# Which softmax heads VectorE computes: a fixed list per head group, or two heads of a key tile ahead when counted time allows

## The chip, the cores and the metric

The kernel runs on one core of one Trainium2 chip. The metric is device time in microseconds (us), from one execution's start to its end on the device; lower is better. "The time" is the median of several executions; a profile shows one execution.

## The reference

Four layers in a row on x of shape (1, 2048, 640) in bf16: attention, token mixer, attention, token mixer, each with a layer norm in front and a residual sum behind. Both attention layers use the same weights, both mixers too.

```python
def _A_ref(x, wqkv, wo):                     # attention, H = 32 heads, Dh = 20
    qkv = (x @ wqkv).reshape(B, S, 3, H, Dh) # then transposed to q, k, v of (B, H, S, Dh)
    scores = einsum("bhqd,bhkd->bhqk", q, k) * (Dh ** -0.5)
    o = einsum("bhqk,bhkd->bhqd", softmax(scores), v)
    return o.transpose(...).reshape(B, S, D) @ wo

def _B_ref(x, w1, b1, w2, b2):               # mixes along the 2048 tokens, F = 1536
    u = gelu(einsum("bsd,sf->bdf", layernorm(x), w1) + b1)
    return (einsum("bdf,fs->bds", u, w2) + b2).transpose(0, 2, 1)

x = x + A(layernorm(x)); x = x + B(layernorm(x)); x = x + A(layernorm(x)); x = x + B(layernorm(x))
```

With 32 heads and 2048 x 2048 scores a head, each attention layer has 134 million exponentials.

## The kernel before

**Tiling.** The 32 heads lie in 8 groups `g` of 4 heads `j`, each padded from 20 to 32 columns, so that a group fills 128 partitions. The queries are cut into 4 blocks `qb` of 512, the keys into 16 tiles `kt` of 128. A *unit* is one (qb, g, kt): 4 heads, each a 128 x 512 block of scores (keys on the partitions, queries along the row). A layer has 512 units and 2048 such heads; they are worked through in the order qb, g, kt. A unit's four score matmuls (line 468) use 32 rows of TensorE each; the four matmuls of exp(scores) with V (line 704, with a column of ones for the softmax's denominator) use 32 columns each and add up in one PSUM accumulator `acc` over the group's 16 key tiles.

**Tiles for ScalarE.** Heads for ScalarE are packed into tiles of three and two heads in turn, each width with one PSUM buffer (`sps`). One activation (line 499) computes the exponentials of a tile and writes `P` to SBUF.

**Heads for VectorE.** Some heads go to VectorE instead. Their scores land in a PSUM buffer of their own (`Dt`, one buffer). VectorE computes the exponential for two heads at a time: one read of each head from PSUM (line 346, `ew`), and then a chain of four instructions on both (lines 387 `ey`, 393 `et`, 400 and 405 `Pd`): the fraction's polynomial, and the exponent added as bits. Which heads these are is fixed: `on_ve(n, j)` names all four heads of the group's last key tile, and heads 2 and 3 of the last but one in the first query block and in 11 of the 24 other groups. That is 166 heads a layer.

**The order of the work.** The program is written tile by tile in one Python loop, and all matmuls are chained in that order on TensorE. For each tile `t` the loop emits the scores of tile t+1 (`emit_S`, with `ve_admit` at its end, which may add one VectorE head), the activation of tile t, up to two units' P x V (`pv_next`, `emit_PV`), then "fills": matmuls of other work from `fill_queue`, such as the projections of K and Q, the output projection and the first half of the mixer for finished query blocks. Where too little is left for TensorE, zero matmuls are added (`keep_busy`, line 489). At the end of a step `ve_step` moves a *counted clock* on by the tile's counted length (1.344 or 0.92 us) and emits the VectorE chain's next instructions as far as that clock lets them start. Every VectorE instruction adds its counted duration through `dve_cost`. Nothing of this is measured while the kernel runs: it only fixes the order of the instructions.

- `ve_admit(t)` takes the next head of the fixed list at the earliest every second tile (`VE_SPACING`). In the first query block a group's heads are taken only once the group has started, later from 24 ScalarE heads ahead (`VE_LEAD`). A backlog of over 3.6 us (`VE_BACKLOG`), or a `Dt` that is not yet read by the counted clock, holds it back, unless the heads are `urgent`, near the group's end.
- `pv_next` takes plain units first and the mixed ones (those with VectorE heads) at the group's end.
- `ve_flush` emits what is left of a unit's chain when its P x V is emitted.
- After a group's last P x V, `normalize` reads the accumulator (line 507, a 32 x 32 block transpose), takes the reciprocals (510), multiplies (512) all 32 columns of each head's block by them into `T2`, and transposes back into `attnT` (514). The next group's P x V starts two tiles later (`ACC_REST`); it needs the same accumulator buffer.
- A fill's result is copied out of PSUM by VectorE (663 for K and Q, 578 for the mixer, 610 to 648 for the output projection). The mixer's results go from `ustg` (two buffers) to memory by DMAs from the GpSimd queue (581, and 583 with accumulation).

The two mixer stages lie between and behind the attention layers and are not touched.

## Time and profile before

| what | value |
|---|---|
| three runs | 2001.93, 2007.28, 2008.22 us; median 2007.28 |
| the profiled execution | 2002.34 us, of which its span 2000.5 |
| busy, share of the span | TensorE 91%, ScalarE 90%, VectorE 70%, GpSimd 8% |
| first attention stage, 49 to 918 us | 869 us; ScalarE 854.48, VectorE 629.59 busy |
| between: mixer and projections, 918 to 1047 us | 129 us |
| second attention stage, 1047 to 1917 us | 870 us; ScalarE 851.20, VectorE 623.10 busy |
| exponentials on ScalarE (499) | 1506 instructions, 1718.6 us busy, 33.1 us idle before them |
| exponentials on VectorE (346, 387, 393, 400, 405) | 332 heads, 947.4 us busy |
| granted TensorE clock | 0.992 |

The span runs from the first to the last instruction of the profiled execution. Busy time is the union of an engine's instructions. A busy TensorE is partly the zero matmuls, and matmuls of different rows or columns of the array overlap. Idle time "before" a group is what the engine stood idle just ahead of these instructions, with the work that ended the longest part of it.

### The profile page before, as it was taken

What the parts mean: (1) busy time and instruction counts of PE and PEld (TensorE: products, weight loads), DVE (VectorE), ACT (ScalarE), POOL (GpSimd) and SP (SyncE); (2) the same over time, 40 slices, a digit from 0 to 9 for tenths busy, and PEclk for the clock granted to TensorE, in tenths of its full rate; (3) what the DMA queues carried; (4) which work ended last, traced back from release to release, by engine and by line L of the source; (5) the groups of instructions that cost most, each with busy time, mean ns of one, the idle gap of its engine ahead of it and who ended that gap; (6) DMA issues with size and microseconds to landing.
All of it is one profiled execution on the core that took longest, in us unless ns stands there. A gap on an engine that the chain in (4) does not pass through costs nothing.

```text
span 2000.5 us, 41377 instructions
## 1 busy us (share of the span) xinstructions
PE 1819.5 (91%) x17472; PEld 619.9 (31%) x17472; DVE 1399.3 (70%) x2091; ACT 1810.2 (90%) x1644; POOL 155.1 (8%) x220
## 2 busy tenths in 40 slices
PE   7999999999999999897999989999999998998979
PEld 4222222322222222223542222323222222322235
DVE  6777787766776577773667787877657765767742
ACT  5999999999999999996349999999999999999952
POOL 2000000100021001100000000001000310111000
PEclk9999999999999999999999999999999999999989
DMA  6000001200143012314620000112001520222055
GB/s 136 2 1 1 1 21 35 81 26 9 33 84 53 1 46 46 45 15 141 205 85 1 1 1 1 47 39 77 13 21 56 77 38 2 71 52 39 7 154 183
DMA packets 90777, 97.47 MB, mean 49 GB/s; under 512 B 9696, under 2 KB 68192, under 8 KB 90592
## 3 DMA queue, kind: packets, MB, share of 16 engines
q1 hardware_dynamic: 70464, 71.22, 11.5%
q0 software_dynamic: 20128, 23.62, 7.6%
q8 instruction: 136, 2.23, 0.5%
q14 instruction: 49, 0.40, 0.1%
HBM read 55.48 MB, written 39.32 MB: 47 GB/s over the span
## 4 chain that ended last, share of the span: by engine, by line
ACT 29%; issue 25%; DVE 21%; PE 20%; POOL 3%; DMA 2%; SPq 0%; POOLq 0%; ACTq 0%; DVEq 0%
ACT P L499 29%; PE y L943 5%; PE S L468 4%; DVE et L393 3%; DVE ew L346 3%; DVE Pd L400 3%; DVE Pd L405 2%; PE acc L704 2%; POOL uacc L583 2%; PE misc L245 2%; PE acc L489 2%; DVE ey L387 2%; PE pp L236 1%; DVE T L507 1%; DVE KT L663 1%
## 5 line engine op out<-in xcount | busy, mean ns | idle before, releaser
L499 ACT ACTIVATE P<-S 128x1536 bf16<-128x1536 f32 (+1 forms) x1506 | 1718.6, 1311 | 33.1 <-PE S L468 27.2
L468 PE MATMUL S<-QTq,KT 32*128 32x512 bf16 x3764 | 593.3, 383 | 85.5 <-ACT P L499 75.0
L489 PE MATMUL acc<-zr,zw 128*32 128x512 bf16 x6112 | 484.2, 384 | 0.0
L346 DVE TENSOR_SCALAR ew<-Dt 128x512 int32<-128x512 f32 x332 | 226.3, 682 | 286.9 <-PE Dt L468 279.0
L704 PE MATMUL acc<-P,Vaug 128*32 128x512 bf16 x3764 | 383.4, 390 | 22.1 <-DVE T L507 21.5
L468 PEld LDWEIGHTS <-KT 32*128 32x128 bf16 x4096 | 192.5, 91 | 652.4 <-issue 631.6
L393 DVE SCALAR_TENSOR_TENSOR et<-ey 128x1024 f32<-128x1024 f32 x166 | 202.5, 1220 | 4.1
L400 DVE SCALAR_TENSOR_TENSOR Pd<-et,ey 128x1024 bf16<-128x1024 f32 x166 | 202.0, 1217 | 2.7
L405 DVE SCALAR_TENSOR_TENSOR Pd<-ew,Pd 128x1024 int16<-128x1024 int16 x166 | 201.9, 1216 | 2.6
L704 PEld LDWEIGHTS <-Vaug 128*32 128x32 bf16 x4096 | 108.6, 93 | 268.9 <-issue 264.6
L489 PEld LDWEIGHTS <-zw 128*32 128x32 bf16 x6112 | 140.7, 96 | 124.2 <-issue 75.3
L187 POOL TENSOR_TENSOR rstd<-veps,mhalf 128x1 f32<-128x1 f32 x64 | 38.9, 608 | 1248.3 <-DVE veps L182 1127.2
L468 PE MATMUL Dt<-QTq,KT 32*128 32x512 bf16 x332 | 126.7, 382 | 6.4 <-DVE ew L346 5.7
L572 PE MATMUL misc<-h2st,w1st 128*128 128x512 bf16 (+1 forms) x576 | 115.3, 302 | 10.1 <-DVE ustg L578 9.4
L578 DVE COPY ustg<-misc 128x512 f32<-128x512 f32 (+1 forms) x144 | 69.4, 482 | 76.9 <-PE misc L572 39.2
L387 DVE TENSOR_SCALAR ey<-ew 128x1024 f32<-128x1024 uint16 x166 | 114.7, 691 | 3.4
L583 POOL DMA_DIRECT2D uacc<-ustg x96 | 86.2, 908 | 346.7 <-DVE ustg L578 318.7
L943 PE MATMUL y<-uT,w2s 128*128 128x512 bf16 (+1 forms) x768 | 107.9, 299 | 2.6 <-ACT uT L886 2.6
L245 PE MATMUL misc<-hh,wq_pad 128*128 128x512 bf16 x310 | 94.2, 384 | 8.6 <-DVE KT L663 6.1
L245 PE MATMUL misc<-hh,wk_pad 128*128 128x512 bf16 x280 | 83.8, 383 | 7.5 <-DVE KT L663 7.4
L507 DVE STREAM_TRANSPOSE T<-acc 128x512 f32<-128x512 f32 x64 | 45.4, 710 | 57.3 <-PE acc L704 57.0
L600 PE MATMUL misc<-wo_pad,attnT 128*128 128x512 bf16 (+1 forms) x384 | 76.1, 303 | 0.5 <-DVE xin L610 0.2
(89 smaller groups left out, 959.2 us busy)
## 6 DMA issues: line engine op xcount, KB each, us to landing
uacc<-ustg POOLq DMA_DIRECT2D x72, 256.0 KB, 4.1
w2s<-in_B_w_dram SPq DMA_DIRECT2D x16, 768.0 KB
w1st<-in_B_w_dram SPq DMA_DIRECT2D x36, 256.0 KB
x1in<-xd SPq DMA_DIRECT2D x24, 320.0 KB
ua<-uacc SPq DMA_DIRECT2D x24, 320.0 KB
xd<-x2s SPq DMA_DIRECT2D x16, 320.0 KB
xin<-xd SPq DMA_DIRECT2D x16, 320.0 KB
uacc<-ustg POOLq DMA_DIRECT2D x72, 64.0 KB, 3.1
```

The source lines that it names most:

```text
L245: pe(nc.tensor.matmul(t[:, :], lhsT=wpad[:, dt_, g, :], rhs=st.hT[:, dt_, tb * 512:(tb + 1) * 512], start=(dt_ == 0), stop=(dt_ == NDT - 1)))
L346: nc.vector.tensor_scalar(out=ve_w[p][:, slot, :], in0=Dt[:, :], scalar1=ve_scale * 65536.0, scalar2=-127.0 * 65536.0, op0=ALU.mult, op1=A ...
L387: nc.vector.tensor_scalar(out=y[:, 0:512 * k], in0=frac, scalar1=EXP_K / 65536.0, scalar2=EXP_K * (1.0 - EXP_ROOT), op0=ALU.mult, op1=ALU.add)
L393: nc.vector.scalar_tensor_tensor(out=box["t"][:, 0:512 * k], in0=y, scalar=EXP_P, in1=y, op0=ALU.add, op1=ALU.mult)
L400: nc.vector.scalar_tensor_tensor(out=box["P"], in0=box["t"][:, 0:512 * k], scalar=EXP_Q, in1=box["y"][:, 0:512 * k], op0=ALU.add, op1=ALU. ...
L405: nc.vector.scalar_tensor_tensor(out=bits, in0=whole, scalar=128.0, in1=bits, op0=ALU.mult, op1=ALU.add)
L468: pe(nc.tensor.matmul(out_ap, lhsT=KT[32 * j:32 * j + 32, g, kt * 128:(kt + 1) * 128], rhs=get_QT(st, qb)[32 * j:32 * j + 32, g, :], start ...
L489: pe(nc.tensor.matmul(acc[32 * j:32 * j + 32, :], lhsT=zw[:], rhs=zr[:].to_broadcast([128, 4, 128]), start=False, stop=False, skip_group_c ...
L499: nc.scalar.activation(out=P[:, 0:ncs, :].rearrange("p a b -> p (a b)"), in_=St[:, 0:ncs, :].rearrange("p a b -> p (a b)"), func=ACT.Exp, ...
L583: nc.gpsimd.dma_start(out=dst, in_=stg[:, 0:w], accum_op=ALU.add)
L704: pe(nc.tensor.matmul(acc[32 * j:32 * j + 32, :], lhsT=Vaug[:, (kt * H + hh) * VW:(kt * H + hh) * VW + 32], rhs=P[:, slot, :], start=(done ...
L943: pe(nc.tensor.matmul(y[:, 0:w], lhsT=w2s[:, ft, sl * 128:(sl + 1) * 128], rhs=uT[:, ft, c0:c1], start=(ft == 0), stop=(ft == NF - 1)))
```

## The change

The list of VectorE's heads is no longer fixed. `on_ve` now asks a dictionary that is filled while the program is written, and the tiles are built one at a time (`take_acts`), skipping heads that VectorE has taken.

- `ve_admit` takes a pair of heads from a unit seven ahead of the one that the tiles have reached (`VE_AHEAD`), if the counted clock allows it: spacing, backlog and `Dt` as before, at most four pairs under way, and the unit's K and Q not waiting in the fill queue. There is no urgent case. The pair's second head comes from the same unit.
- VectorE's exponential instructions are counted at their duration divided by 0.92 (`VE_DUTY`).
- `ve_step` holds the chain while the pair three before is not yet used, since `Pd` has three buffers.
- `pv_next` goes through the group's units in order. A unit with VectorE heads is passed over until it is ready by the counted clock, or three tiles have passed (`VE_LATE`).
- `normalize` multiplies 20 of the 32 columns of each block; `T2` is one buffer a layer, zeroed once by GpSimd. Its counted cost goes from 2.4 to 2.15 us.

```diff
-    VE_LEAD=24,
...
-    VE_URGENT=26,
+    VE_AHEAD=7,
+    VE_LATE=3,
+    VE_DUTY=0.92,
...
+            T2 = ntmp.tile([128, 16, 32], BF16, name="T2")
+            nc.gpsimd.memset(T2[:], 0.0)
...
             def on_ve(n, j):
-                qb, g, kt = units[n]
-                return kt == NKT - 1 or (kt == NKT - 2 and j >= 2 and (qb == 0 or (g % 2 == 0 and qb + g > 1)))
...
+                return (n, j) in on_dve
+
+            def take_acts(t):
+                acts = []
+                while len(acts) < 3 - t % 2 and cursor[0] < NCH:
+                    n, i = divmod(cursor[0], len(HORDER))
+                    cursor[0] += 1
+                    if i == 0:
+                        starts.setdefault(t, []).append(n)
+                    if on_ve(n, HORDER[i]):
+                        continue
+                    loc[(n, HORDER[i])] = (t, len(acts))
+                    last_tile[n] = t
+                    acts.append((n, HORDER[i]))
...
             def ve_admit(t):
-                if not ve_left or t - ve_state["last"] < CFG["VE_SPACING"]:
+                if cursor[0] >= NCH or t - ve_state["last"] < CFG["VE_SPACING"]:
                     return
...
+                backlog = max(0.0, ve_clock["free"] - ve_clock["now"]) + sum(c[1] for c in ve_chain)
+                if ve_state["slot"] == 0 and ve_state["pair"] - 4 in ve_users:
+                    return
+                if backlog > CFG["VE_BACKLOG"] or ve_state["read"] > ve_clock["now"]:
+                    return
+                if ve_state["slot"] == 0:
+                    n = max(cursor[0] // len(HORDER) + CFG["VE_AHEAD"], ve_state["unit"] + 1)
+                    if n >= NU or {("K", units[n][1]), ("Q",) + units[n][0:2]} & pending_keys():
                         return
...
+                    ve_state["unit"] = n
+                n = ve_state["unit"]
                 js = {c[1] for c in tiles[t]}
...
+                free = [j for j in HORDER if not on_ve(n, j)]
+                c = (n, next((j for j in free if j not in js), free[0]))
+                on_dve[c] = True
                 ve_state["last"] = t
-                if units[c[0]][0:2] != units[tiles[t][0][0]][0:2]:
-                    ensure_ready(*units[c[0]][0:2])
                 ve_first(c)
...
             def ve_next():
                 p, cost, fn = ve_chain.popleft()
                 fn()
-                dve_cost(cost)
+                dve_cost(cost / CFG["VE_DUTY"])
...
                 while ve_chain and ve_clock["free"] <= ve_clock["now"] + CFG["VE_SLACK"]:
+                    if ve_chain[0][0] - 3 in ve_users and ve_chain[0][1] > 1:
+                        break
                     ve_next()
...
-                T2 = ntmp.tile([128, 16, 32], BF16, name="T2")
-                nc.vector.tensor_tensor(out=T2[:], in0=T1v,
-                                        in1=rden[:].unsqueeze(2).to_broadcast([128, 16, 32]), op=ALU.mult)
+                nc.vector.tensor_tensor(out=T2[:, :, 0:DH], in0=T1v[:, :, 0:DH],
+                                        in1=rden[:].unsqueeze(2).to_broadcast([128, 16, DH]), op=ALU.mult)
...
-                    dve_cost(2.4)
+                    dve_cost(2.15)
...
+                pending = pv_pending[pv_group]
+                for n in pending:
+                    if not located(n) or last_tile[n] > t - LAGT:
+                        break
+                    if not ve_need(n) or ve_done(n) or last_tile[n] <= t - CFG["VE_LATE"]:
+                        pending.remove(n)
+                        return n
```

More of the change, by code (lines that the diff above doesn't have):

```diff
@@ L294, in attention @@
             HORDER = (0, 1, 2, 3)
-            def on_ve(n, j):
-                qb, g, kt = units[n]
-                return kt == NKT - 1 or (kt == NKT - 2 and j >= 2 and (qb == 0 or (g % 2 == 0 and qb + g > 1)))
-            chunks = [(n, j) for n in range(NU) for j in HORDER]
-            tiles, loc, last_tile = [], {}, {}
-            act_chunks = deque(c for c in chunks if not on_ve(*c))
-            ve_left = deque(sorted((c for c in chunks if on_ve(*c)), key=lambda c: (c[0] // NKT, -c[0], c[1])))
@@ L304, in attention @@
-            first_act = {}
-            for i, c in enumerate(act_chunks):
-                first_act.setdefault(c[0] // NKT, i)
-            act_end = {g_: i for g_, i in ((k - 1, v) for k, v in first_act.items())}
-            acts_before = []
-            taken = 0
-            while act_chunks:
-                t = len(tiles)
-                acts = [act_chunks.popleft() for _ in range(min(3 - t % 2, len(act_chunks)))]
-                acts_before.append(taken)
-                taken += len(acts)
-                for i, c in enumerate(acts):
-                    loc[c] = (t, i)
-                    last_tile[c[0]] = t
-                tiles.append(acts)
@@ L319, in attention @@
-            act_end[NU // NKT - 1] = taken
-            for n in range(NU):
-                last_tile.setdefault(n, -1)
-            NTILES = len(tiles)
-            tile_left = {t: len(acts) for t, acts in enumerate(tiles)}
-            pv_count = {}
-            pv_plain = [deque() for _ in range(NU // NKT)]
-            pv_mixed = [deque() for _ in range(NU // NKT)]
-            for n in range(NU):
-                (pv_mixed if any(on_ve(n, j) for j in HORDER) else pv_plain)[n // NKT].append(n)
@@ L329, in attention @@
-            for q_ in pv_mixed:
-                q_.reverse()
-            ve_w, ve_P, ve_ready = {}, {}, {}
+            NCH = NU * len(HORDER)
+            GCH = NKT * len(HORDER)
+            cursor = [0]
+            starts = {}
+            on_dve = {}
+            tiles, loc, last_tile, tile_left = [], {}, {}, {}
+            pv_count = {}
+            pv_pending = [list(range(g_ * NKT, (g_ + 1) * NKT)) for g_ in range(NU // NKT)]
+            def on_ve(n, j):
+                return (n, j) in on_dve
@@ new lines, in take_acts @@
+            def take_acts(t):
[10 more added lines that the diff above has]
+                    acts.append((n, HORDER[i]))
+                if acts:
+                    tile_left[t] = len(acts)
+                    tiles.append(acts)
+                return acts
@@ L332, in attention, with located @@
+            def located(n):
+                return cursor[0] >= len(HORDER) * (n + 1)
+            ve_w, ve_P, ve_ready, ve_users = {}, {}, {}, {}
             ve_chain = deque()
             ve_clock = dict(now=0.0, free=0.0)
-            ve_state = dict(last=-9, pair=0, slot=0, read=0.0)
+            ve_state = dict(last=-9, unit=-1, pair=0, slot=0, read=0.0)
             def dve_cost(us):
@@ L341, in ve_first @@
                 loc[c] = (p, slot)
+                ve_users.setdefault(p, []).append(c)
                 Dt = dps.tile([128, 512], F32, name="Dt")
@@ L347, in ve_first @@
                                         scalar2=-127.0 * 65536.0, op0=ALU.mult, op1=ALU.max)
-                dve_cost(0.69)
+                dve_cost(0.69 / CFG["VE_DUTY"])
                 ve_state["read"] = ve_clock["free"]
                 ve_state["slot"] = 1 - slot
-                if slot == 1 or not ve_left:
-                    ve_enqueue(p, slot + 1)
+                if slot == 1:
+                    ve_enqueue(p, 2)
                     ve_state["pair"] = p + 1
             def ve_admit(t):
-                if not ve_left or t - ve_state["last"] < CFG["VE_SPACING"]:
+                if cursor[0] >= NCH or t - ve_state["last"] < CFG["VE_SPACING"]:
@@ L357, in ve_admit @@
                     return
-                grp_ = ve_left[0][0] // NKT
-                if grp_ < NG:
-                    if acts_before[t] < first_act[grp_]:
-                        return
-                elif acts_before[t] < first_act[grp_] - CFG["VE_LEAD"]:
-                    return
-                left = sum(1 for c in ve_left if c[0] // NKT == grp_)
-                urgent = act_end[grp_] - acts_before[t] < CFG["VE_URGENT"] + 6 * left
-                backlog = max(0.0, ve_clock["free"] - ve_clock["now"]) + sum(c[1] for c in ve_chain)
@@ L367, in ve_admit @@
-                if not urgent and (backlog > CFG["VE_BACKLOG"] or ve_state["read"] > ve_clock["now"]):
-                    return
+                backlog = max(0.0, ve_clock["free"] - ve_clock["now"]) + sum(c[1] for c in ve_chain)
[6 more added lines that the diff above has]
+                    if n >= NU or {("K", units[n][1]), ("Q",) + units[n][0:2]} & pending_keys():
+                        return
+                    ve_state["unit"] = n
@@ L369, in ve_admit @@
+                n = ve_state["unit"]
                 js = {c[1] for c in tiles[t]}
-                same = [c for c in ve_left if c[0] == ve_left[0][0]]
-                c = next((c for c in same if c[1] not in js), same[0])
-                ve_left.remove(c)
+                free = [j for j in HORDER if not on_ve(n, j)]
+                c = (n, next((j for j in free if j not in js), free[0]))
+                on_dve[c] = True
                 ve_state["last"] = t
-                if units[c[0]][0:2] != units[tiles[t][0][0]][0:2]:
-                    ensure_ready(*units[c[0]][0:2])
@@ L419, in ve_step @@
                 while ve_chain and ve_clock["free"] <= ve_clock["now"] + CFG["VE_SLACK"]:
+                    if ve_chain[0][0] - 3 in ve_users and ve_chain[0][1] > 1:
+                        break
                     ve_next()
             def ve_need(n):
-                return {loc[(n, j)][0] if (n, j) in loc else -1 for j in HORDER if on_ve(n, j)}
+                return {loc[(n, j)][0] for j in HORDER if on_ve(n, j)}
             def ve_done(n):
                 need = ve_need(n)
-                return (-1 not in need and not any(c[0] in need for c in ve_chain) and
+                return (not any(c[0] in need for c in ve_chain) and
                         all(ve_ready.get(p) is not None and ve_ready[p] <= ve_clock["now"] for p in need))
             def ve_flush(n):
-                while -1 in ve_need(n):
-                    c = next(c for c in ve_left if c[0] == n)
-                    ve_left.remove(c)
-                    ve_first(c)
                 need = ve_need(n)
@@ L472, in emit_S @@
             def emit_S(t):
-                for (n, j) in tiles[t]:
-                    if j == HORDER[0]:
-                        on_unit_start(n)
+                for n in starts.get(t, ()):
+                    on_unit_start(n)
                 w = 3 - t % 2
@@ L707, in emit_PV @@
                                         tile_position=(0, 32 * j)))
-                    if not on_ve(n, j):
+                    if on_ve(n, j):
+                        ve_users[ti].remove((n, j))
+                        if not ve_users[ti]:
+                            del ve_users[ti]
+                    else:
                         tile_left[ti] -= 1
@@ L762, in pv_next @@
             def pv_next(t, n_pv):
-                if pv_group >= len(pv_plain) or t < pv_start:
+                if pv_group >= len(pv_pending) or t < pv_start or n_pv == 2:
                     return None
-                plain, mixed = pv_plain[pv_group], pv_mixed[pv_group]
-                if plain and last_tile[plain[0]] <= t - LAGT and n_pv < 2:
-                    return plain.popleft()
-                if mixed and last_tile[mixed[0]] <= t - LAGT and len(plain) < NKT - 3 and n_pv < 2:
-                    if not plain or (n_pv == 0 and ve_done(mixed[0])):
-                        return mixed.popleft()
+                pending = pv_pending[pv_group]
[5 more added lines that the diff above has]
+                        return n
                 return None
@@ L778, in attention @@
             hist = deque(maxlen=2)
+            take_acts(0)
             emit_S(0)
-            for t in range(NTILES):
+            t = -1
+            while t + 1 < len(tiles):
+                t += 1
                 has_fill = planned_fill()
-                if t + 1 < NTILES:
+                more = len(take_acts(t + 1))
+                if more:
                     emit_S(t + 1)
@@ L787, in attention @@
                 step_us = 0.92 if short else 1.344
-                next_us = 0.92 if t + 1 < NTILES and len(tiles[t + 1]) < 3 else 1.344
-                own = 0.25 * (len(tiles[t + 1]) if t + 1 < NTILES else 0) + 0.25 * (ve_state["last"] == t + 1)
+                next_us = 0.92 if more < 3 else 1.344
+                own = 0.25 * more + 0.25 * (ve_state["last"] == t + 1)
                 while (n := pv_next(t, n_pv)) is not None:
-                    if len(pv_plain[pv_group]) + len(pv_mixed[pv_group]) == 0:
+                    if not pv_pending[pv_group]:
                         want = wanting(hist, own + n_pv + 1 + (1.0 if has_fill else 0), step_us, 0.6, next_us)
@@ L795, in attention @@
                     n_pv += 1
-                    if not pv_plain[pv_group] and not pv_mixed[pv_group]:
+                    if not pv_pending[pv_group]:
                         pv_group += 1
@@ L806, in attention @@
             in_attention[0] = False
-            while (n := pv_next(NTILES + 9, 0)) is not None:
+            while (n := pv_next(len(tiles) + 9, 0)) is not None:
                 emit_PV(n)
-                if not pv_plain[pv_group] and not pv_mixed[pv_group]:
+                if not pv_pending[pv_group]:
                     pv_group += 1
```

## The prediction

> **What bounds the kernel now.** I read the page's busy times first, then busy time by stage, then the groups kept apart by shape, then the waits, and last the timeline around the longest waits.

> ```profile
> PE 1819.5 (91%) x17472; PEld 619.9 (31%) x17472; DVE 1399.3 (70%) x2091; ACT 1810.2 (90%) x1644; POOL 155.1 (8%) x220
> 49.00:918.00 869.00, 797.90 (x7920) 247.86 (x7918) 629.59 (x861) 854.48 (x749) 64.75 (x84) 1.00 0.14 29
> 1047.00:1917.00 870.00, 801.07 (x7917) 247.40 (x7915) 623.10 (x854) 851.20 (x747) 64.22 (x84) 0.99 0.14 31
> ```

> The first line is the whole span; the others are the two attention stages (length, then PE, PEld, DVE, ACT and POOL busy, granted clock, DMA share, GB/s). In them ScalarE is busy 854.48 of 869 us and 851.20 of 870 us, VectorE 72%. TensorE's 92% is no bound: 484.2 us of its work are the zero matmuls of L489, which the planner puts in by count.

> ```profile
> L499 ACT ACTIVATE P<-S 128x1536 bf16<-128x1536 f32 (+1 forms) x1506 | 1718.6, 1311 | 33.1 <-PE S L468 27.2
> L346 DVE TENSOR_SCALAR ew<-Dt 128x512 int32<-128x512 f32 x332 | 226.3, 682 | 286.9 <-PE Dt L468 279.0
> L393 DVE SCALAR_TENSOR_TENSOR et<-ey 128x1024 f32<-128x1024 f32 x166 | 202.5, 1220 | 4.1
> L400 DVE SCALAR_TENSOR_TENSOR Pd<-et,ey 128x1024 bf16<-128x1024 f32 x166 | 202.0, 1217 | 2.7
> L405 DVE SCALAR_TENSOR_TENSOR Pd<-ew,Pd 128x1024 int16<-128x1024 int16 x166 | 201.9, 1216 | 2.6
> L387 DVE TENSOR_SCALAR ey<-ew 128x1024 f32<-128x1024 uint16 x166 | 114.7, 691 | 3.4
> L512 DVE TENSOR_TENSOR T<-T,rden 128x512 bf16<-128x512 f32 x64 | 43.9, 685 | 1.3
> ```

> Busy time and mean ns stand behind the first bar, idle time before the group behind the second. ScalarE's exponentials fill the attention stages but for 33.1 us of idle time. VectorE computes 332 heads (a head is one 128x512 block of scores) and stands idle 279.0 us before L346 because no head has been given to it. So the time goes down with each head that leaves ScalarE, as long as VectorE's queue makes nobody late.

> ```profile
> PE S L468 <- ACT P L499: 75.0, 285, 1.0
> DVE ustg L578 <- DMA uacc<-ustg: 34.8, 12, 4.4
> ACT P L499 <- PE S L468: 27.2, 69, 1.7
> PE acc L704 <- DVE T L507: 21.5, 39, 1.2
> ```

> Sum, times and longest wait. TensorE waits for ScalarE more often than the other way round. Two waits lead to VectorE: TensorE's for the accumulator, which L507 must read first, and VectorE's own for a DMA, which stops its whole queue.

> **The change, part by part.**

> *Price of a head.* On ScalarE 1718.6 us / 3764 heads (L468 S x3764) = 0.4566 us; tiles stay three and two heads wide, so a head that leaves shortens the row of tiles by this much. On VectorE (226.3 + 202.5 + 202.0 + 201.9 + 114.7) / 332 = 2.854 us. TensorE does the same matmuls for a head in either place.

> *How many heads move.* Before it is fixed: 166 a layer (128 of key tile 15, 16 + 22 of key tile 14). After, the counted clock decides. A pair of heads is counted at (2 x 0.69 + 0.69 + 3 x 1.22) / 0.92 = 6.23 us, a tile at (1.344 + 0.92) / 2 = 1.132 us. In a quiet stretch the rule falls into a rhythm: after the second head of a pair has been taken at tile k, the backlog shows 5.5, 4.4 and 3.8 us at k+1 to k+3, all above 3.6, and 2.6 at k+4, where the next pair's first head is taken; its second follows at k+6. A pair thus takes 6 tiles or 6.79 us, and 6.23 / 6.79 = 92% of the counted time is used. Now a layer: some 744 tiles x 1.132 = 842 us, less what else is counted on VectorE: normalization 32 x 2.15 = 68.8, K and Q copies 59 x 0.69 = 40.7, the staged mixer copies 3 x 11.64 = 34.9, output projection 12 + 16, layer norm 12 x 1.6 = 19.2, together 191.6. The remaining 650 us hold 104 pairs at 6.23 and 96 at the rhythm's 6.79. Two pairs more go: in the last 7 key tiles no tile lies ahead (some 11 us, 1.7 pairs), and in the first query block the next group's keys are still in the fill queue for part of each group. That leaves 94 pairs, 188 heads, 22 more than now; 1860 heads / 2.5 = 744 tiles agrees with the start. Bounds: 104 pairs (208) if no counted time is lost; about 172 if the copies, which cut the rhythm, cost another tenth of it. I take 188, since the rhythm comes straight from the rule.

> *Worth.* 2 x 22 x 0.4566 = 20.1 us off ScalarE, which is the path. Bounds from the counts: 2 x 6 x 0.4566 = 5.5 and 2 x 42 x 0.4566 = 38.4 us.

> *VectorE's load.* Per layer + 22 x 2.854 = 62.8 us. The normalization of 320 instead of 512 columns lies between 685 ns (nothing saved) and 685 x 320 / 512 = 428 ns; the rows of 512 and 128 columns of the same operation (L648: 687 and 284 ns) give 150 ns + 1.05 ns a column, so 486 ns, 0.2 us less, 6.4 us a layer. Together about 627 - 6 + 63 = 684 of some 860 us, 80%. Neither lies on the path while VectorE has a fifth of its time left. The zeroing of T2 is one POOL instruction a layer, which stands idle there (x0 in the stage's first 198 us); its nearest row is POOL's L187 at 608 ns, and nobody waits for it until the first normalization, 28 us later.

> *Is a pair ready in time?* From the first head: backlog up to 3.6, two reads at 0.75, the chain 4.73, and a normalization (2.15) and a copy (0.69) between, 12.7 us counted. Seven key tiles are 28 heads, some 10 tiles, and the sums of P and V come two tiles later: 12 x 1.132 = 13.8 us. The margin is thin, but counted time is 8% longer than real time on VectorE's side, and for three tiles TensorE takes other key tiles first. If it is missed, TensorE stops before L704 with the next tiles' scores behind it, and ScalarE waits for these.

> *Waits at the group's end.* In the first query block VectorE is now idle when a group ends, and L507 starts 0.05 us after the last matmul in seven of eight groups; in most of the later ones it stands behind a running instruction, and TensorE waits 21.5 us in 39 places. With VectorE evenly loaded the 16 groups of the two layers' first blocks join them: 16 x 0.55 = 9 us more at most. Against it, the urgent heads go: in these same groups the tiles take 1.1 to 2.0 us a group longer than ScalarE's undisturbed pace (1.33 and 0.90 us a tile), 0.4 to 0.9 in quiet groups, so about 16 x 0.7 = 11 us may come back. Bounds for waits as a whole: half of the 33.1 us gone (-16), or 12 us added. Between them I take + 2, since TensorE's copies must now also pass a fuller VectorE queue.

> [...] POOL's issue at L583 takes 862 ns in the median and 1.16 us in the first of these lines, beside a running L387 (start, length, engine):

> ```profile
> 806.38 1.16 POOL L583 DMA_DIRECT2D uacc<-ustg  x1 [3.81 <-DVE ustg L578]
> 806.72 0.74 DVE L387 TENSOR_SCALAR ey<-ew 128x1024 f32<-128x1024 uint16 x1
> 809.22 0.86 POOL L583 DMA_DIRECT2D uacc<-ustg  x1 [1.67 <-DVE ustg L578]
> ```

> [...]

> *Sum.* - 20.1 + 2 = - 18 us. The profiled execution took 2002.34 us (span 2000.5 and 1.84 around it), so it would take 1984; the median of the three runs, 2007.28, lies 4.9 above it, so I forecast 1989.

> **The rivals.**

> *Smoother still* (0.13). The bursts of urgent heads, not the number of heads, made most of ScalarE's waits; half of 33.1 us goes as well: 2007.3 - 20.1 - 16.5 = 1971. For it: the longest of these waits (0.9 us) stand where a Dt matmul waits for L346 in a burst. Against: most follow the accumulator wait, which stays.

> *It takes no more heads* (0.12). If the copies break the rhythm more than I reckon, the rule ends near 166 to 175 heads and the gain is under 2 x 9 x 0.4566 = 8 us, which 2 us of waits bring to 6: 2001 to 2007. For it: 85% instead of 92% use of the counted time gives it already. About 0.3% (6 us) is what a measurement of this kernel can tell from no change.

> *VectorE's stops for the DMA reach ScalarE* (0.13, slower). L578 has two buffers and waits 34.8 us for the accumulating DMA (median 4.1 us to landing). With VectorE 72% busy little comes through: after the stops of 3.98 and 3.05 us near 798 and 805 us ScalarE lost 0.50 + 0.17 + 0.67 = 1.34 us. With the queue always full, L346 and L507 behind such a stop hold TensorE. All of it coming through costs 34.8 - 20.1 = + 14.7 us, 2022; it outweighs the gain from 20.1 / 34.8 = 58%, where 19% comes through now.

> **How the numbers follow.** The forecast's own case has 0.62; with the first rival, faster holds 0.74 (0.01 given to a weak gain), same 0.13, slower 0.13. The range runs from 1972 (first rival, or 200 heads a layer) to 2006 (the second rival's bulk), and leaves out the third and the far ends, 0.18.

> **What would show it.** L346 with about 376 instructions instead of 332, L499 near 1488 instructions and 1698 us; VectorE near 80% in the attention stages and L346's idle time down by more than 100 us; L512 near 486 ns; the stages some 9 us shorter each. Wrong would be: L346 at 350 or fewer; ScalarE's idle time before L499 above 50 us; a row of TensorE waiting at L704 for VectorE's L405; the DMA wait of L578 well above 34.8 us.

## The result, and the profile after

| | before | after |
|---|---|---|
| median of 6 runs, us | 2005.1 (2001.9 to 2009.0) | 1979.5 (1974.0 to 1983.8) |
| profiled execution, its span | 2002.34, 2000.5 | 1980.09, 1978.3 |
| heads on VectorE | 332 | 360 |
| tiles on ScalarE | 1506 | 1494 |

The changed kernel takes 25.6 us less; the ratio is 0.987, its 95% interval 0.985 to 0.9891.

Busy times of the changed kernel, then its two attention stages from the first to the last exponential (start and end, length, then PE, PEld, DVE, ACT and POOL busy, granted clock, DMA share, GB/s):

```profile
PE 1771.2 (90%) x17158; PEld 617.7 (31%) x17352; DVE 1481.8 (75%) x2175; ACT 1790.8 (91%) x1632; POOL 158.4 (8%) x222
47.00:915.00 868.00, 783.44 (x7832) 248.02 (x7914) 671.35 (x903) 849.57 (x747) 65.94 (x84) 0.99 0.13 29
1030.00:1893.00 863.00, 779.86 (x7831) 248.02 (x7911) 671.26 (x903) 849.91 (x748) 65.23 (x84) 0.99 0.14 32
```

The bounds 49 to 918 and 1047 to 1917 us, by which the stages before were given, are not quite the first and last exponential: measured from these, the stages took 873.7 and 877.5 us before, and take 867.1 and 862.6 now. Together they fall by 21.5 us. ScalarE is still what the stages are made of. VectorE is at 671 of some 865 us, 77 to 78%. The groups that answer to those shown of before, first of the page and then (the last line) kept apart by shape:

```profile
L495 ACT ACTIVATE P<-S 128x1536 bf16<-128x1536 f32 (+1 forms) x1494 | 1699.2, 1330 | 31.1 <-PE S L465 24.0
L347 DVE TENSOR_SCALAR ew<-Dt 128x512 int32<-128x512 f32 x360 | 247.0, 686 | 203.1 <-PE Dt L465 190.3
L392 DVE SCALAR_TENSOR_TENSOR et<-ey 128x1024 f32<-128x1024 f32 x180 | 219.9, 1222 | 5.1
L404 DVE SCALAR_TENSOR_TENSOR Pd<-ew,Pd 128x1024 int16<-128x1024 int16 x180 | 219.3, 1218 | 3.9
L507 DVE TENSOR_TENSOR T<-T,rden 128x320 bf16<-128x320 f32 x64 | 31.1, 487 | 1.4
```

The heads' instructions on VectorE cost what they did, within 1% (L347 686 ns against 682, L392 1222 against 1220, L404 1218 against 1216), and ScalarE's 1699.2 us for 3736 heads are 0.4548 us each against 0.4566. 28 heads have moved, VectorE (L347, L346 before) waits 84 us less for heads (203.1 against 286.9), and the normalization of 20 columns takes 487 ns against 685. The waits:

```profile
PE S L465 <- ACT P L495: 91.9, 343, 0.9
ACT P L495 <- PE S L465: 24.0, 33, 2.7
DVE ustg L573 <- DMA uacc<-ustg: 22.8, 20, 3.1
PE acc L699 <- DVE T L503: 7.8, 20, 1.0
PE misc L567 <- DVE h2st L193: 5.8, 2, 2.9
PE misc L630 <- DVE attnT L509: 4.9, 4, 1.9
```

The last two are new: in the kernel before, TensorE has no such waits in the attention stages. Its wait for the accumulator has gone from 21.5 us in 39 places to 7.8 in 20. ScalarE's idle time is nearly what it was, but in other portions: before, 69 waits for scores of at most 1.7 us, now 33 of up to 2.7 us.

**A common account.** A busy sum doesn't show all waiting, since an activation can start late while the one before it still counts as busy: before, the activation of a tile of three heads counts as busy for 1.52 us in the mean, but the next starts 1.33 us after it in the median. So I measure both attention stages in another way: from the start of each activation to the start of the next. Undisturbed, that is 1.330 us for a tile of three heads and 0.904 for one of two (the medians before). The sum of these is the *pace*; what the starts take beyond it is the *excess*.

| kernel | heads | median us (ratio to before, 95%) | pace | excess | half clock |
|---|---|---|---|---|---|
| before | 332 | 2005.1 | 1680.0 | 68.7 | 13.7 |
| after | 360 | 1979.5 (0.985 to 0.9891) | 1666.6 | 59.8 | 30.7 |
| e1, spread evenly | 332 | 1989.8 (0.9899 to 0.9932) | 1680.0 | 52.6 | 6.8 |
| e2, 32 columns | 360 | 1985.5 (0.9872 to 0.9908) | 1666.6 | 61.5 | 34.1 |
| e3, before with 20 columns | 332 | 2006.2 (0.9986 to 1.0012) | 1680.0 | 69.2 | 13.7 |
| e4, later fills | 360 | 1967.1 (0.9789 to 0.9834) | 1666.6 | 44.5 | 6.8 |
| e5, duty 0.85 | 352 | 2000.6 (0.9953 to 0.9979) | 1671.0 | 74.2 | 41.0 |
| e6, duty 1.04 | 388 | 1975.3 (0.9818 to 0.9862) | 1655.8 | 63.6 | 20.5 |
| e7, buffers apart | 360 | 1977.3 (0.9828 to 0.987) | 1666.6 | 51.5 | 20.5 |
| e8, e4 + e7, duty 1.04 | 392 | 1958.7 (0.9725 to 0.9776) | 1653.2 | 47.9 | 3.4 |
| e9, before with later fills | 332 | 2014.8 (1.0029 to 1.0063) | 1680.0 | 74.4 | 17.1 |
| e10, e1 + e4 | 332 | 1980.0 (0.9854 to 0.9882) | 1680.0 | 44.1 | 0 |
| e11, e4 + e7, duty 1.12 | 400 | 1950.3 (0.9709 to 0.9734) | 1648.6 | 44.7 | 3.4 |
| e12, e4 + e7, duty 1.2 | 416 | 1967.6 (0.9793 to 0.9818) | 1642.4 | 68.7 | 27.3 |

Pace, excess and half clock (the time in the stages for which the records grant TensorE half its clock) are sums over both layers of one profiled execution each; medians are over 4 to 12 runs. The kernel before, run beside each set, had medians of 2005.1 to 2006.5.

In the change itself the span falls by 22.2 us: 13.4 of pace and 8.9 of excess. So the gain has two parts, and the second stood in my sum with the other sign, as + 2.

**The new stops.** The excess is not spread evenly any more. Groups of 16 key tiles with over 2 us of excess make 27 us of the 59.8, in seven places: the 10th, 11th, 21st and 31st group of the first layer, and the 11th, 20th and 31st of the second. The largest, in the timeline of the changed kernel (start, length, engine, line; in brackets the idle time before it):

```profile
333.40 1.51 ACT L495 ACTIVATE P<-S 128x1536 bf16<-128x1536 f32 x1
334.06 1.22 DVE L404 SCALAR_TENSOR_TENSOR Pd<-ew,Pd 128x1024 int16<-128x1024 int16 x1
334.24 1.46 POOL L188 TENSOR_TENSOR rstd<-veps,mhalf 128x1 f32<-128x1 f32 x1 [10.54 <-DVE veps L183]
335.73 0.61 DVE L193 TENSOR_SCALAR h2st<-x1s,mv,rstd 128x640 bf16<-128x640 f32 x1 [0.44 <-POOL rstd L188]
336.40 0.59 PE L567 MATMUL misc<-h2st,w1st 128*128 128x512 bf16 x1 [2.92 <-DVE h2st L193]
336.92 0.61 PE L465 MATMUL S<-QTq,KT 32*128 32x512 bf16 x2
337.62 1.02 ACT L495 ACTIVATE P<-S 128x1024 bf16<-128x1024 f32 x1 [2.71 <-PE S L465]
```

The first staged mixer matmuls (L567) need the layer norm's result `h2st`, and one of them waits for it. The norm's small instructions stand in VectorE's queue between those of a pair's chain, and its GpSimd step (L188, 0.55 us in the median) takes 1.46 us beside L404. TensorE waits 2.92 us with the next scores (L465) behind L567, and ScalarE 2.71. Then comes the second half of the price, in the changed kernel's stretches around it:

```profile
320.00:333.00 13.00, 12.13 (x116) 3.97 (x116) 10.46 (x22) 12.82 (x12) 0.55 (x1) 1.00 0.23 74
336.00:343.00 7.00, 6.60 (x45) 1.57 (x45) 1.76 (x4) 3.80 (x4) 1.16 (x2) 0.53 0.12 47
343.00:350.00 7.00, 6.33 (x57) 2.02 (x60) 5.08 (x8) 7.00 (x7) 1.08 (x2) 1.00 0.28 84
```

The granted clock is 0.53 in the 7 us from the end of the stop, a score matmul takes 0.61 us instead of 0.39, and ScalarE is busy 3.80 of 7 us. Most of the other places are alike: at 310.40 us an output projection waits 1.33 us for a copy (L605), at 864.66 us the first partial output projection waits 1.93 us for `attnT` (L509), at 601.72 a mixer matmul waits 1.85 us for a copy that waits for the DMA. At 1547 us in the second layer half clock begins 1.1 us after a wait of only 0.61 us for L503 at a group's end, and 16 of the planner's zero matmuls (L485), 1.90 us long at half clock, stand ahead of the next scores. In the profiled executions before and after, a clock of one half is granted for 3.413, 6.827 or 10.240 us at a time, but for a last stretch that ends with the span (3.125 and 2.725 us).

### The profile page after: what moved, and what is told of

It is laid out like the page before. It is cut to its first block, busy times and chain, and to the rows that moved or that the text cites. A ratio compares the mean times of both kernels' runs of the same rounds, so it can differ in the third digit from the quotient of the medians.

```text
span 1978.3 us, 40960 instructions
## 1 busy us (share of the span) xinstructions
PE 1771.2 (90%) x17158; PEld 617.7 (31%) x17352; DVE 1481.8 (75%) x2175; ACT 1790.8 (91%) x1632; POOL 158.4 (8%) x222
## 3 DMA queue, kind: packets, MB, share of 16 engines
q1 hardware_dynamic: 70464, 71.22, 11.6%
## 4 chain that ended last, share of the span: by engine, by line
ACT 47%; issue 22%; PE 18%; DVE 10%; POOL 2%; DMA 2%; POOLq 0%; DVEq 0%; ACTq 0%
ACT P L495 47%; PE y L947 5%; PE S L465 3%; PE acc L699 2%; PE acc L485 2%; PE pp L237 1%; DVE et L392 1%; DVE Pd L399 1%; POOL uacc L578 1%; PE misc L246 1%; DVE ew L347 1%; DMA uacc<-ustg 1%; PE misc L595 1%; PE big L876 1%; DVE Pd L404 1%
## 5 line engine op out<-in xcount | busy, mean ns | idle before, releaser
L495 ACT ACTIVATE P<-S 128x1536 bf16<-128x1536 f32 (+1 forms) x1494 | 1699.2, 1330 | 31.1 <-PE S L465 24.0
L465 PE MATMUL S<-QTq,KT 32*128 32x512 bf16 x3736 | 593.6, 384 | 113.9 <-ACT P L495 91.9
L485 PE MATMUL acc<-zr,zw 128*32 128x512 bf16 x5992 | 470.9, 385 | 0.9
L465 PEld LDWEIGHTS <-KT 32*128 32x128 bf16 x4096 | 198.3, 91 | 667.6 <-issue 644.7
L699 PE MATMUL acc<-P,Vaug 128*32 128x512 bf16 x3736 | 394.7, 390 | 8.9 <-DVE T L503 7.8
L347 DVE TENSOR_SCALAR ew<-Dt 128x512 int32<-128x512 f32 x360 | 247.0, 686 | 203.1 <-PE Dt L465 190.3
L392 DVE SCALAR_TENSOR_TENSOR et<-ey 128x1024 f32<-128x1024 f32 x180 | 219.9, 1222 | 5.1
L399 DVE SCALAR_TENSOR_TENSOR Pd<-et,ey 128x1024 bf16<-128x1024 f32 x180 | 219.3, 1218 | 4.1
L404 DVE SCALAR_TENSOR_TENSOR Pd<-ew,Pd 128x1024 int16<-128x1024 int16 x180 | 219.3, 1218 | 3.9
L485 PEld LDWEIGHTS <-zw 128*32 128x32 bf16 x5992 | 133.3, 96 | 130.2 <-issue 84.4
L699 PEld LDWEIGHTS <-Vaug 128*32 128x32 bf16 x4096 | 100.0, 93 | 226.7 <-issue 223.0
L188 POOL TENSOR_TENSOR rstd<-veps,mhalf 128x1 f32<-128x1 f32 x64 | 40.1, 628 | 1353.5 <-DVE veps L183 1241.3
L465 PE MATMUL Dt<-QTq,KT 32*128 32x512 bf16 x360 | 139.2, 387 | 2.7 <-DVE QTq L658 1.8
L386 DVE TENSOR_SCALAR ey<-ew 128x1024 f32<-128x1024 uint16 x180 | 124.2, 690 | 4.1
L567 PE MATMUL misc<-h2st,w1st 128*128 128x128 bf16 (+1 forms) x508 | 101.1, 294 | 19.6 <-DVE ustg L573 9.8
L947 PE MATMUL y<-uT,w2s 128*128 128x128 bf16 (+1 forms) x754 | 106.8, 297 | 4.0 <-ACT uT L890 3.3
L578 POOL DMA_DIRECT2D uacc<-ustg x96 | 87.0, 925 | 275.9 <-DVE ustg L573 249.2
L595 PE MATMUL misc<-wo_pad,attnT 128*128 128x128 bf16 (+1 forms) x363 | 72.2, 300 | 5.5 <-DVE x1s L605 2.3
L947 PEld LDWEIGHTS <-w2s 128*128 128x128 bf16 x768 | 59.7, 98 | 49.8 <-issue 5.0
```

What stands on the lines that cost most here:

```text
L347: nc.vector.tensor_scalar(out=ve_w[p][:, slot, :], in0=Dt[:, :], scalar1=ve_scale * 65536.0, scalar2=-127.0 * 65536.0, op0=ALU.mult, op1=A ...
L386: nc.vector.tensor_scalar(out=y[:, 0:512 * k], in0=frac, scalar1=EXP_K / 65536.0, scalar2=EXP_K * (1.0 - EXP_ROOT), op0=ALU.mult, op1=ALU.add)
L392: nc.vector.scalar_tensor_tensor(out=box["t"][:, 0:512 * k], in0=y, scalar=EXP_P, in1=y, op0=ALU.add, op1=ALU.mult)
L399: nc.vector.scalar_tensor_tensor(out=box["P"], in0=box["t"][:, 0:512 * k], scalar=EXP_Q, in1=box["y"][:, 0:512 * k], op0=ALU.add, op1=ALU. ...
L404: nc.vector.scalar_tensor_tensor(out=bits, in0=whole, scalar=128.0, in1=bits, op0=ALU.mult, op1=ALU.add)
L465: pe(nc.tensor.matmul(out_ap, lhsT=KT[32 * j:32 * j + 32, g, kt * 128:(kt + 1) * 128], rhs=get_QT(st, qb)[32 * j:32 * j + 32, g, :], start ...
```

## Experiments

Theory A: heads and waits both count, and part of the waits are the new stops. Its rivals stand in the expectations.

**e1: the same number of heads as before, spread evenly.** In `ve_admit`, ahead of the choice of a unit:

```diff
+                if ve_state["slot"] == 0 and len(on_dve) * NCH >= 166 * (cursor[0] + 28):
+                    return
```

> The changed kernel with a cap: a pair is taken only while VectorE's heads are fewer than 166 of 2048 of the heads reached, so 332 heads as before the change, but spread evenly. Theory A (the heads taken and the quieter waits both count): the 28 heads cost 28 x 0.4566 = 12.8 us, so about 1992, half way to the 2005 of before. Theory B (the number of heads is all): about 2005. Theory C (evenness is all): about 1980.

1989.8 us. Neither B nor C: with 332 heads, as before, taking them evenly in this order is worth 15.5 us, and the excess falls from 68.7 to 52.6. Of these 16.1 us 11.6 lie in the two layers' first query blocks, counted up to the eighth group's L503: 23.2 us of excess there before, 11.6 in e1, 11.2 after. The other six blocks have 45.5, 41.0 and 48.6. e1 keeps all else of the change, too: heads taken seven key tiles ahead, no urgent case, the new order of P x V. That evenness alone does it is not shown.

**e2 and e3: the normalization alone, taken out and put in.**

```diff
-                nc.vector.tensor_tensor(out=T2[:, :, 0:DH], in0=T1v[:, :, 0:DH],
-                                        in1=rden[:].unsqueeze(2).to_broadcast([128, 16, DH]), op=ALU.mult)
+                nc.vector.tensor_tensor(out=T2[:], in0=T1v,
+                                        in1=rden[:].unsqueeze(2).to_broadcast([128, 16, 32]), op=ALU.mult)
```

> The changed kernel with the normalization over all 32 columns again, everything else in the same order. Theory A: VectorE gets 64 x 0.2 = 13 us more work off the path, so within 2 us of the changed kernel (1980 to 1982). Rival D (VectorE's queue is on the path at the groups' ends): up to 13 us slower, 1985 to 1993.

> The kernel before with the normalization of 20 columns alone, counted at 2.15 us. Theory A: 2003 to 2006, no difference that can be measured. Rival D: up to 13 us faster, 1992 to 2000.

e3 shows nothing (0.9986 to 1.0012): in the kernel before, these columns lie off the path. e2's median is 6 us above the changed kernel's, more than A said, and at the lower end of D's range; but the intervals of the ratios overlap, and in the profiles pace and excess together are 1.7 us apart, the rest of the difference lying outside the attention stages, where e2 changes nothing. So this difference stays open: D's full 13 us do not show in either run, a part of them is not excluded with 360 heads.

**e4: later fills.** The first pair of lines is for the staged mixer matmuls, the second for the partial output projections.

```diff
-                            fill_queue.append(dict(..., key=("M", p), dve=...))
+                            fill_queue.append(dict(..., key=("M", p), not_before=fill_state["unit"] + 4, dve=...))
...
-                                          not_before=fill_state["unit"] + 2))
+                                          not_before=fill_state["unit"] + 4))
```

> The changed kernel with two waiting times in the fill queue made longer: the staged mixer matmuls start 4 units after the layer norm is put in the queue (at once in the changed kernel), the last block's partial output projections 4 units after the normalization (2 in the changed kernel). Heads stay 360. Theory A with the stops (TensorE waits 2.9 and 1.9 us for VectorE at these places, then runs at half clock for 3.4 to 6.8 us, and ScalarE loses 4 to 5 us at each): three to four of the seven such places go, 8 to 14 us faster, 1966 to 1972. Rival E (ScalarE would have lost this anyway, at the next accumulator wait): within 3 us of 1980.

1967.1, 12.5 us faster. The waits of L567 for L193 and of L630 for L509 are gone from the attention stages, the excess is 44.5, and half clock is down from 30.7 to 6.8 us. E is refuted. ScalarE's group on e4's page:

```profile
L495 ACT ACTIVATE P<-S 128x1536 bf16<-128x1536 f32 (+1 forms) x1494 | 1698.6, 1335 | 16.5 <-PE S L465 12.0
```

With the same 1494 tiles it stands idle 16.5 us, where it was 31.1.

**e9 and e10: the later fills on the kernel before, and on e1.**

> The kernel before with the same two longer waiting times in the fill queue as in the later fills. Theory A (TensorE's stops at the first staged mixer matmul and at the partial output projection came with the change's fuller VectorE queue): little to win before, 2001 to 2006. Rival J (they were there all along): about 12 us faster, 1993.

> The capped kernel (332 heads, evenly spread) with the later fills. Theory A (the price of a head and the stops add up): 28 x 0.4566 = 12.8 us above the later fills' 1967, so 1980. Rival K (with fewer heads these stops are hardly there, as only two stretches at half clock in the capped kernel suggest): 1985 to 1990, no faster than without the later fills by more than 4 us.

On the kernel before the later fills lose 9 us, where A said no change and J a gain. So the stops came with the change's order: before, there is no wait to take away at these places, and in e1, with as few heads, TensorE waits 1.7 us for `h2st` and 2.4 us for `attnT`. Why it loses: VectorE's wait for the DMA and TensorE's for the accumulator grow, in the waits of e9 from 34.8 and 21.5 us to

```profile
DVE ustg L578 <- DMA uacc<-ustg: 51.0, 18, 4.8
PE acc L704 <- DVE T L507: 26.4, 44, 1.3
```

which fits fills pushed onto the bursts of heads; that is argued, not tested. e10 falls where A put it, and K is refuted: between e10 and e4 only the number of heads differs, 28 heads for 13.0 us, 0.46 us each. With e1 there are four corners: the later fills give 9.7 us at 332 heads and 12.5 at 360. Without the later fills the same 28 heads give 10.2 us.

**e5 and e6: fewer and more heads.** `VE_DUTY` at 0.85 and at 1.04.

> The changed kernel with VectorE's exponentials counted at their duration divided by 0.85 instead of 0.92: 352 heads instead of 360. Theory A (each head is worth 0.4566 us, waits as they were): 8 x 0.4566 = 3.7 us slower, 1983. Rival G (a less loaded VectorE makes fewer stops): no slower than 1980.

> The same with 1.04: 388 heads, VectorE some 83% busy in the attention stages. Theory A: 28 x 0.4566 = 12.8 us faster than the changed kernel, 1967. Rival G: more and longer stops of TensorE eat it up, 1975 or above.

Both miss A. e5 should have lost 3.7 us and lost 21: 4.4 us of pace and 14.4 of excess, with 41.0 us at half clock. e6 gained 4 instead of 12.8: pace - 10.8, excess + 3.8, and the rest outside the attention stages. G says the reverse of what e5 shows. e6's 1975.3 lies in G's range, but its half clock is 20.5 us, less than after, so the stops that G named are a part of the loss at most. In e5 several stops are at other places than after: at 218 and 679 us half clock begins at a group's end, behind a wait for L503 of only 0.57 and 0.68 us. So the number of heads alone does not set the stops. That it is which instruction meets which in VectorE's queue, and that each new order throws the stops elsewhere, fits these runs but was not tested by itself. What makes one order worse than another I can't say from these runs.

**e7: the staged copies' narrow and wide buffers apart.**

```diff
+            ustn = p1.enter_context(tc.tile_pool(name=f"ustn{layer}", bufs=2))
...
-                                stg = ustg.tile([128, 512], F32, name="ustg")
+                                stg = (ustg.tile([128, 512], F32, name="ustg") if w > 256 else
+                                       ustn.tile([128, 128], F32, name="ustn"))
```

> The changed kernel with buffers of their own for the narrow staged copies (two of 512 columns, two of 128), so that a copy waits for a DMA issued twice as long ago. The order stays. VectorE waits 22.8 us for this DMA now, and one of TensorE's stops (1.85 us before L567, then 6.8 us at half clock in the first layer) comes from it. Theory A: that wait goes, 3 to 7 us faster, 1972 to 1977. Rival H (VectorE's slack hides the DMA wait anyway): within 2 us of 1980.

1977.3: 2.2 us faster by the medians, between A's range and H's, so the time doesn't decide between them. The wait for the DMA has left the list of its longest waits, the stop near 600 us is gone (0.5 instead of 5.1 us of excess in its group), and the excess is 8 us smaller in the profiled execution, whose span is 3.2 us shorter.

**e8, e11, e12: all of it, and more heads.**

> The later fills, the buffers apart and 1.04 together: 392 heads. Theory A: 1967 for the later fills, less 32 x 0.4566 = 14.6, less some 3 for the buffers: 1948 to 1952. Rival G: the fuller VectorE makes new stops, 1960 or above.

> Later fills, buffers apart, durations divided by 1.12: 400 heads. Theory A: 8 x 0.4566 = 3.7 us below the 1958.7 of 1.04, so 1955. Rival G (VectorE full, new stops): 1960 or above.

> The same with 1.2: 416 heads, VectorE some 88% busy in the attention stages, and counted as faster than it is. Theory A: 24 x 0.4566 = 11 us below 1958.7, so 1948. Rival G: 1960 or above.

e8 came to 1958.7, some 7 us above A's range and 1.3 below G's, e11 to 1950.3, below its 1955: the fastest here, 2.8% under the kernel before. From e10 to e11 (which has the buffers apart as well) the pace falls by 31.4 us and the time by 29.7, with 68 more heads and nearly the same excess. e12 turns back to 1967.6, as G had it. The attention stages of e11 (two lines) and e12 (two lines):

```profile
47.00:895.00 848.00, 773.09 (x7849) 245.16 (x7934) 722.08 (x964) 839.45 (x739) 64.86 (x84) 1.00 0.14 30
1015.00:1864.00 849.00, 774.80 (x7863) 245.02 (x7947) 721.84 (x963) 841.12 (x740) 64.61 (x84) 1.00 0.15 32
```

```profile
47.00:904.00 857.00, 780.25 (x7784) 243.19 (x7870) 745.08 (x987) 837.76 (x736) 64.86 (x84) 0.99 0.14 30
1025.00:1881.00 856.00, 776.47 (x7777) 242.61 (x7857) 745.27 (x989) 835.43 (x734) 64.86 (x84) 0.99 0.15 33
```

VectorE is 85% busy in e11 and 87% in e12, and the excess goes from 44.7 to 68.7. The worst place in e12, between 135 and 141 us, begins with a wait for the accumulator: L504 stands behind the chain and TensorE is idle for 1.09 us, then runs at half clock for 6.8 us.

## Why the prediction was right, and where it was not

**The time.** 1989 was forecast, within 1972 to 2006 and faster at 0.74; it is 1979.5. ScalarE bounds the stages, a head that leaves is worth its 0.46 us where the waits stay alike (0.4566 by the busy time, 0.46 between e10 and e4), and VectorE's queue can carry more: these steps hold. Two terms were mis-sized, in opposite senses: pace and excess fell by 22 us where the sum had 18, while the terms were off by 7 and 11. That the sum came so near is in part luck. Another 2.2 us lie in the base: the three runs known then had a median of 2007.3, the six now have 2005.1.

**How many heads move: 188 a layer forecast, 180 measured.** The failing step is the rhythm of a quiet stretch taken for the whole layer. A new pair begins after 6 tiles in only 17 of 89 cases of the first layer; 8 is commonest (27), and 10 or 11 come 19 times. VectorE's other work (copies, normalizations, layer norm) breaks it: between two pairs 6 tiles apart it did 0.1 us of other work in the mean, 8 tiles apart 1.9, and 10 or 11 apart 4.1. So the second rival had it, only half as far (it needed 166 to 175). By query blocks the profile has 46, 47, 46 and 41 heads. So the term was 2 x 14 x 0.4566 = 12.8 us instead of 20.1; the pace fell by 13.4.

**Waits: + 2 forecast, - 9 measured.** One part held: without the urgent heads some 11 us were to come back in the two layers' first query blocks, and the excess there fell by 12.0 us (11.6 in e1). The failing step is the 9 us set against it. L503 was to stand behind a running instruction in these 16 groups as well; TensorE's wait for the accumulator rose there only from 0.6 to 1.6 us. In the other 48 groups, where the sum left it alone, it fell from 20.9 to 6.2 us (12.6 in e1). ScalarE got nothing of that in the change itself, because the stops came into these blocks: their excess is 45.5 us before and 48.6 after. The "smoother still" rival saw that more comes back, but the stops took back two thirds of it: without most of them (e4) the excess is 33.3 us in these blocks and 24 us below that of before in all.

**Is a pair ready in time?** Yes: no wait of L699 for L404 is in the changed kernel's list.

**POOL beside VectorE.** Of 96 issues of L578 (L583 before) 25 now meet a running L386 (L387 before, where 15 did). Ten of these take 1.16 to 1.47 us (nine before, likewise), against 0.865 us in the median of all, and the group's busy time grew by 0.8 us (86.2 to 87.0): off the path. L188 was on it: in the changed kernel four of its 64 instructions run beside a SCALAR_TENSOR_TENSOR (L404), and each takes 1.46 us, where the median is 0.55; at 334 us that is some 0.9 of the 2.92 us of the stop. In the kernel before, four had taken 1.39 to 1.46 us beside L405. What makes them longer no run here shows. I had reckoned with the DMA issues alone.

**VectorE's stops for the DMA reach ScalarE.** The wait fell to 22.8 us, and one stop comes from it, in the first layer, with 5.1 us of excess in its group (0.5 in e7). The rival named a real mechanism but the wrong size, and not the main one: the stops that come in both layers are waits of TensorE for VectorE's short instructions at places where the fill queue asks for their result at once.

**The normalization.** 487 ns against 486 reckoned, and in the kernel before nothing that can be measured in the time (e3); with 360 heads up to 6 us stay open (e2).

**What would show it.** L346 was to have 376 instructions and has 360, L499 some 1488 and 1698 us and has 1494 and 1699.2. The stages were to be 9 us shorter each and are 6.6 and 14.9. L346's idle time was to fall by more than 100 us and fell by 84, VectorE to reach 80% and reached 77 to 78: both fit the 8 heads a layer that didn't move.

## What to carry to other kernels

Where one engine's queue is filled by count, work out how far the count's rhythm survives the other work in that queue before multiplying by it, and expect the order in which a load comes to be worth as much as its amount: here 15.5 us for the same heads in another, more even order. When a queue is made fuller, look for the places where another engine asks for a result of that queue at once, short instructions included (here TensorE's waits of 2.92 us at L567 and 1.93 us at L630), and put them later; here two changed numbers gave 12.5 us. Then raise the load until the stops come back (here between 85% and 87% busy), not before.

## What I had not expected of the hardware

In the changed kernel the stops of TensorE cost more than their length. Stops of 1.85, 1.93 and 2.92 us each came with 3.4 to 6.8 us at half clock, in which ScalarE lost again: after its first wait of 1.46 us (at 602 us) come 1.34, 0.60 and 0.98, after 1.99 (at 865 us) 0.92, and at 336 us, of 5.3 us of excess in the group, 2.7 are the wait itself. And 16 of the planner's zero matmuls take 1.90 us (after, at 1547 us), 20 of them 2.31 us (e5, at 680 us), in front of the scores once the clock has fallen; 12 take 1.47 us at half clock and 0.83 at full clock (after, at 865.6 and 868.7 us).

Over the fourteen kernels the excess stays within 44 to 53 us where half clock takes under 7 us, and lies between 51 and 74 above that. The runs don't separate what the clock costs from what the stops ahead of it cost.
